# Two-bank PSUM tiles in a fused attention and rational feed-forward kernel on one Trainium2 core

## The chip, the cores and the metric

The kernel runs on one core of one Trainium2 chip. The metric is the device time of one execution in microseconds; lower is better. Three runs of the kernel before gave 1387.79, 1389.79 and 1392.57 us, median 1389.79. The profile is that of one further execution.

The engines are named as the profile names them: PE multiplies matrices (PEld is its load of the stationary operand), DVE is the vector engine, ACT the scalar engine, POOL the general engine that cannot see PSUM, SP issues the DMAs. PSUM is the buffer that PE writes into: eight banks of 512 fp32 a partition.

## The reference

Causal attention by blocks of 64, for 8 batches of 8 heads with 576 positions of 64 elements, then a feed-forward layer over the 4608 tokens of 512 elements (2048 hidden), whose nonlinearity is a quotient of two polynomials:

```python
scores = scale * np.matmul(q, k.transpose(0, 1, 3, 2))
mask = block_i >= block_j                      # blocks of 64 positions
scores = np.where(mask, scores, -1000000000.0)
scores = scores - np.max(scores, axis=-1, keepdims=True)
attn = np.exp(scores)
attn = attn / (np.sum(attn, axis=-1, keepdims=True) + 1e-09)
attn_out = np.matmul(attn, v)

h = x @ w_in
P = a[0] + a[1] * h + a[2] * h2 + a[3] * h3    # h2 = h*h, h3 = h2*h
Q = 1.0 + np.abs(b[0]) * np.abs(h) + np.abs(b[1]) * h2
out = (P / (Q + 1e-6)) @ w_out
```

## The kernel before

**Number format.** All operands of the matmuls are fp32r. Each is split into a high part, rounded by ACT, and a low part, the rest, mostly subtracted by DVE or POOL; a product is three matmuls (low x high, high x high, high x low), for scores two over a contraction of 128 rows in which both parts are stacked.

**Order.** The program is traced in one order, by hand, and the framework's planner then fixes the order of every engine's queue at build time, from a simulated timeline and the buffers that are free in it. On the chip each queue is executed in that fixed order, each instruction waiting for its semaphores. So an instruction that is traced late can run early: the first weight block is traced at step 9 but starts at 14 us in the trace.

**Attention.** The unit is a pair of heads, 32 in all; `load(p)` brings q, k and v. `prep(p, which)` transposes q or k (six transposes of 96 rows, L354, in two groups of three, each in its own bank), copies the high part with ACT (L358) and subtracts the low part with DVE (L359); DMAs then lay `kq` out for each head. `vprep(p)` splits v into `vpad`, where 64-column blocks of the two heads lie with gaps of zeros: four ACT copies and four POOL subtractions (L381, L382), two of them for the first 64 keys and two over 256 columns.

The queries are cut into five tiles `t` of 64, 128, 128, 128 and 128 rows, whose keys are the first 64, 192, 320, 448 and 576. A step of the loop `attn_steps` is one tile of one head, so a pair takes ten steps and all attention 320:

- `scores(p, t, j)`: two matmuls (L420, L421) and, on the last block, a small one that adds the mask (L424), into a bank of `ps_a`. Tile 4 has 576 columns, more than a bank holds, and is done in two halves of 288 in two banks. DVE takes the negated maximum of each bank (L425); for tile 4 L428 joins the two maxima.
- `expo(p, t, j)`, one step later: ACT's exp with the maximum as bias and the row's sum as accumulator (L437, which shows as an ACTIVATE and a reading of the accumulator), twice for tile 4. With the second head POOL joins tile 4's two sums (L443), adds 1e-9 (L444), DVE inverts (L445), and POOL scales: the first 64 keys of both heads into `pk` (L446), the rest in place in `pt` (L450).
- `transp(p, t)`, nine steps after the tile's second score: 1, 3, 5, 7 or 9 transposes (L469) in groups with a bank each, of sizes 1; 1, 2; 1, 4; 4, 3; 3, 3, 3. ACT copies a group's high part (L474), DVE subtracts the low part (L475). Tile 0 has 64 rows, so its transpose works on 64 rows and its tile `pt` serves as `pk` too.
- `pv(p, g)`, a step after tiles 2 and 4 have been transposed: the second product (15 matmuls over tiles 0 to 2, 27 over tiles 3 and 4, L488) into one bank of `ps_a`, evicted by ACT and DVE (L491, L492) and written to `xscr` in DRAM.

**Banks.** `ps_a` has five banks, `ps_h` one for the hidden activations, `ps_o` two (tags `o0` and `o1`) for the FFN's output. Scores and `pv` always take `ps_a`. Transposes ask `bank(p, ...)`, which for the first four pairs goes round `ps_a`, `o0`, `o1` and `ps_h`, since the FFN isn't running yet, and later takes `ps_a`.

**Weights.** `split_weights` splits the weights in 32 blocks of 128 x 512 with exact integer work: ACT's absolute value (L127), a maximum with a tiny constant on POOL (L128), six DVE operations (L130 to L137), an ACT conversion (L139), a POOL product (L143 or L145). Twenty blocks belong to the first part of the hidden units (phase 0), twelve to the second, kept in DRAM till it starts.

**Feed-forward.** Tokens are taken in 18 blocks of 256, hidden units two at a time: phase 0 has 5 such units a block, phase 1 has 3. `first` is 24 matmuls into a two-part bank h (L200) and the start of the polynomials; `recip` makes the quotient (for phase 1 its reciprocal `r0` is a bank of `ps_a`); `split` the two parts of g; `second` 12 matmuls (L249) that accumulate into `self.o`, two tiles of one bank, over the units of a block. At a block's end phase 0 copies the two halves with ACT (L256) to DRAM; phase 1 adds them to that partial result with two DVE operations (L262) and writes the output. In phase 1, h alternates between `ps_h` and `ps_a`. FFN's units are fed in between the steps of attention from step 53 on, when the first batch is there; what is left runs after attention ends.

## Time and profile before

| what | value |
|---|---|
| median of three runs | 1389.79 us |
| the profiled execution, and its span | 1388.67 us, 1386.9 us |
| mean granted clock of PE | 0.971 |
| PE, PEld busy | 1296.0, 1190.8 us |
| DVE, ACT, POOL busy | 1031.0, 909.3, 958.3 us |
| first matmul of the FFN's h | 133.4 us |
| last score matmul of attention begins | at about 961 us |

The profile's page gives each engine's busy time as a union of its instructions' spans. Matmuls are pipelined, so their spans overlap and a busy PE need not be one at its full rate; the count of matmuls in a stretch of time says more. The page cuts the span in 40 slices of 34.7 us; these are its rows for the engines (tenths of the slice that are busy, 9 standing for 90% or more) and for the clock:

```profile
PE   4778799999899989999999999999989999999998
DVE  5898877787678868877767777766756677777665
POOL 4888987687677757777767676766556655556564
PEclk9687999999999999999999999999999999999999
```

The chain of waits, followed back from the last instruction, is 70% PE, 9% DVE, 8% POOL, 5% ACT and 4% DMA. In the groups of instructions, a row has the line, engine, operation, output and inputs, shapes and count, then the busy time in us, the mean of one in ns, and the idle time of the engine ahead of them with what ended it.

### The profile page before, as it was taken

What the parts mean: (1) busy time and instruction counts of PE and PEld (TensorE: products, weight loads), DVE (VectorE), ACT (ScalarE), POOL (GpSimd) and SP (SyncE); (2) the same over time, 40 slices, a digit from 0 to 9 for tenths busy, and PEclk for the clock granted to TensorE, in tenths of its full rate; (3) what the DMA queues carried; (4) which work ended last, traced back from release to release, by engine and by line L of the source; (5) the groups of instructions that cost most, each with busy time, mean ns of one, the idle gap of its engine ahead of it and who ended that gap; (6) DMA issues with size and microseconds to landing.
All of it is one profiled execution on the core that took longest, in us unless ns stands there. A gap on an engine that the chain in (4) does not pass through costs nothing.

```text
span 1386.9 us, 25820 instructions
## 1 busy us (share of the span) xinstructions
PE 1296.0 (93%) x8736; PEld 1190.8 (86%) x8736; DVE 1031.0 (74%) x2048; ACT 909.3 (66%) x2250; POOL 958.3 (69%) x1240
## 2 busy tenths in 40 slices
PE   4778799999899989999999999999989999999998
PEld 3667788999888889888989999999979999999897
DVE  5898877787678868877767777766756677777665
ACT  5766766777577766776777777776545655555553
POOL 4888987687677757777767676766556655556564
PEclk9687999999999999999999999999999999999999
DMA  9778555666556665675654565651711333333332
GB/s 221 191 195 236 147 150 160 168 168 181 147 136 154 163 167 140 156 171 140 168 134 110 153 149 126 150 141 44 263 55 61 107 122 122 122 122 122 122 122 91
DMA packets 225635, 200.93 MB, mean 145 GB/s; under 512 B 132064, under 2 KB 195552, under 8 KB 225504
## 3 DMA queue, kind: packets, MB, share of 16 engines
q1 hardware_dynamic: 225440, 199.28, 53.8%
q8 instruction: 70, 1.15, 0.3%
q14 instruction: 61, 0.50, 0.1%
q0 software_dynamic: 64, 0.00, 0.0%
HBM read 98.57 MB, written 44.04 MB: 103 GB/s over the span
## 4 chain that ended last, share of the span: by engine, by line
PE 70%; DVE 9%; POOL 8%; ACT 5%; DMA 4%; issue 2%; SPq 1%; POOLq 0%; ACTq 0%; DVEq 0%
PE h L200 25%; PE o L249 25%; PE o L488 9%; PE t L469 4%; PE s L420 3%; PE s L421 3%; PE tp L354 2%; ACT p L437 1%; DVE v L224 1%; POOL u L210 1%; DVE nm L425 1%; POOL p L450 1%; DMA x<-xscr 1%; POOL gl L233 1%; DVE u L223 1%
## 5 line engine op out<-in xcount | busy, mean ns | idle before, releaser
L200 PE MATMUL h<-x,wih 128*128 128x256 f32 x2304 | 442.6, 288 | 10.1 <-DMA x<-xscr 5.9
L200 PEld LDWEIGHTS h<-x,wih 128*128 128x128 f32 x2304 | 368.8, 192 | 19.6 <-issue 6.8
L200 PE MATMUL h<-x,wil 128*128 128x256 f32 x1152 | 329.5, 286 | 0.0
L249 PE MATMUL o<-woh,gl 128*128 128x512 f32 x576 | 233.0, 405 | 8.1 <-POOL gl L233 6.8
L209 POOL TENSOR_SCALAR v<-u,bab 128x512 f32<-128x512 f32 x144 | 119.7, 831 | 162.9 <-ACT u L207 160.8
L249 PE MATMUL o<-woh,gh 128*128 128x512 f32 x576 | 228.5, 397 | 0.0
L249 PE MATMUL o<-wol,gh 128*128 128x512 f32 x576 | 227.2, 395 | 0.0
L233 POOL TENSOR_TENSOR gl<-s,gh 128x512 fp32r<-128x512 f32 x144 | 188.4, 1309 | 51.4 <-ACT gh L232 48.3
L425 DVE TENSOR_REDUCE nm<-s 128x1 f32<-128x288 f32 (+4 forms) x384 | 161.7, 427 | 81.2 <-PE s L424 46.1
L200 PEld LDWEIGHTS h<-x,wil 128*128 128x128 f32 x1152 | 221.3, 192 | 0.5
L437 ACT ACTIVATE p<-s,nm 128x288 f32<-128x288 f32 (+4 forms) x384 | 184.6, 485 | 48.4 <-DVE nm L425 34.9
L210 POOL TENSOR_TENSOR u<-v,u 128x512 f32<-128x512 f32 x144 | 189.7, 1318 | 9.8
L450 POOL TENSOR_SCALAR p<-p,rc 128x128 f32<-128x128 f32 (+3 forms) x256 | 166.2, 660 | 30.0 <-DVE rc L445 28.3
L217 ACT ACTIVATE v<-u,qcb 128x512 f32<-128x512 f32 x144 | 104.6, 726 | 95.9 <-POOL u L210 95.1
L207 ACT ACTIVATE u<-h 128x512 f32<-128x512 f32 x144 | 86.0, 597 | 120.8 <-PE h L200 114.4
L420 PE MATMUL s<-kq 128*128 128x256 f32 (+3 forms) x384 | 138.3, 362 | 22.0 <-DMA kq<-hl 9.6
L211 DVE TENSOR_TENSOR s<-s,h 128x512 f32<-128x512 f32 x144 | 98.6, 684 | 68.7 <-ACT s L208 67.9
L249 PEld LDWEIGHTS o<-woh,gl 128*128 128x128 f32 x576 | 109.5, 190 | 28.9 <-POOL gl L233 9.3
L249 PEld LDWEIGHTS o<-wol,gh 128*128 128x128 f32 x576 | 109.1, 189 | 22.8
L249 PEld LDWEIGHTS o<-woh,gh 128*128 128x128 f32 x576 | 109.5, 190 | 16.0
L421 PE MATMUL s<-kq 128*128 128x256 f32 (+3 forms) x384 | 121.0, 317 | 0.0
L469 PE MATMUL t<-ident,p 128*128 128x128 f32 (+1 forms) x672 | 114.0, 280 | 6.2 <-DVE x L492 1.8
(105 smaller groups left out, 3031.9 us busy)
## 6 DMA issues: line engine op xcount, KB each, us to landing
kq<-hl SPq DMA_DIRECT2D x64, 432.0 KB, 4.2
x<-xscr SPq DMA_DIRECT2D x96, 256.0 KB, 3.6
kq<-hl SPq DMA_DIRECT2D x64, 288.0 KB, 5.3
xscr<-x SPq DMA_DIRECT2D x32, 320.0 KB, 4.2
qr<-in_q_dram SPq DMA_DIRECT2D x64, 144.0 KB, 2.8
kr<-in_k_dram SPq DMA_DIRECT2D x64, 144.0 KB, 2.9
kq<-hl SPq DMA_DIRECT2D x64, 144.0 KB, 4.8
pscr<-os SPq DMA_DIRECT2D x18, 512.0 KB, 3.2
```

The costliest lines, as they stand in the source:

```text
L200: nc.tensor.matmul(h[:, j, :], lhsT=w[:, dc, fs], rhs=xs[dc // 2][:, dc % 2, hl, :], start=(dc == 0 and i == 0), stop=(dc == 3 and i == 2))
L209: nc.gpsimd.tensor_scalar(out=vt, in0=ut, scalar1=b1, scalar2=b0, op0=ALU.mult, op1=ALU.add)
L210: nc.gpsimd.tensor_tensor(out=ut, in0=vt, in1=ut, op=ALU.mult)
L233: nc.gpsimd.tensor_tensor(out=gl.rearrange("p j t -> p (j t)"), in0=st, in1=gh.rearrange("p j t -> p (j t)").bitcast(F32), op=ALU.subtract)
L249: nc.tensor.matmul(self.o[m], lhsT=g[:, j, ms], rhs=w[:, f, :], start=(u == 0 and j == 0 and i == 0), stop=(u == nu - 1 and j == 1 and i = ...
L420: nc.tensor.matmul(ps[:, :ww], lhsT=kq[:, 0, qs], rhs=kq[:, 1, c0:c0 + ww], start=True, stop=False)
L421: nc.tensor.matmul(ps[:, :ww], lhsT=kq[:, 0, qs], rhs=kq[:, 2, c0:c0 + ww], start=False, stop=not last)
L425: nc.vector.reduce_max(out=nm[:nq, j, i:i + 1], in_=ps[:nq, :w], axis=AX.X, negate=True)
L437: nc.scalar.activation(out=pt[:nq, j, c0:c0 + w], in_=banks[i][:nq, :w], func=AF.Exp, bias=nm[:nq, j, 0:1], scale=1.0, accum_out=sm[:nq, j ...
L450: nc.gpsimd.tensor_scalar(out=pt[:nq, jj, 64:n], in0=pt[:nq, jj, 64:n], scalar1=rc[:nq, jj:jj + 1], scalar2=1.0, op0=ALU.mult, op1=ALU.mult)
L469: nc.tensor.transpose(ps[:, i, :nq], src, ident[:nq, :nq])
L488: nc.tensor.matmul(o[:, s0:w], lhsT=vblock(vv, x), rhs=pp, start=(x == 0 and i == 0), stop=(x == nb - 1 and i == 2))
```

## The change

The eight banks are dealt out anew: `ps_a` three banks, a new pool `ps_w` one tile of two banks, `ps_h` one, `ps_o` one tile of two banks. `wide(p, ...)` hands out two-bank tiles: for the first four pairs `ps_w` and `ps_o` in turn, later `ps_w` alone. `bank` goes to `ps_a` three times in four and to `ps_h` once for the first four pairs, and to `ps_a` later.

With that,

- prep's six transposes go into one wide tile, with one ACT copy and one DVE subtraction of 576 columns where there were two of 288;
- tile 4's scores go into one wide tile: one maximum over both banks, one exp with one sum; L428 and L443 go;
- `transp` works in groups of 1; 1, 2; 1, 4; 7; 5, 4, where those of 7 and 5 are wide;
- v's blocks of the two heads are split by one ACT copy and one POOL subtraction of 512 columns;
- tile 0's transpose takes 128 rows, of a tile `p0` that lasts, whose lower half is zeroed once;
- FFN's `self.o` is one tile, copied or added in one operation;
- L128 and L444 on POOL get a second operation that changes nothing (a second maximum with the same constant, a product with 1.0).

```diff
-    ps_a = ctx.enter_context(tc.tile_pool(name="ps_a", bufs=5, space=PSUM))
+    ps_a = ctx.enter_context(tc.tile_pool(name="ps_a", bufs=3, space=PSUM))
+    ps_w = ctx.enter_context(tc.tile_pool(name="ps_w", bufs=1, space=PSUM))
...
-            nc.gpsimd.tensor_scalar_max(at, at, WMIN)
+            nc.gpsimd.tensor_scalar(out=at, in0=at, scalar1=WMIN, scalar2=WMIN, op0=ALU.max, op1=ALU.max)
...
-                self.o = [ps_o.tile([128, DM], F32, name=f"o{ph}_{c}_{m}", tag=f"o{m}")
-                          for m in range(2)]
+                self.o = ps_o.tile([128, 2, DM], F32, name=f"o{ph}_{c}", tag="o")
...
-                    for m in range(2):
-                        nc.scalar.copy(out=osb[:, m, :], in_=self.o[m])
+                    nc.scalar.copy(out=osb, in_=self.o)
...
-                    for m in range(2):
-                        nc.vector.tensor_tensor(out=osb[:, m, :], in0=self.o[m], in1=part[:, m, :], op=ALU.add)
+                    nc.vector.tensor_tensor(out=osb, in0=self.o, in1=part, op=ALU.add)
...
+        p0 = apers.tile([128, 2, 64], F32, name="p0")
+        nc.vector.memset(p0[64:128], 0.0)
...
-            for half in range(2):
-                ps = bank(p - 1, f"tp{p}_{which}_{half}")[:, :3 * LP].rearrange("p (c t) -> p c t", c=3)
...
+            ps = wide(p - 1, f"tp{p}_{which}")
+            for c in range(6):
+                nc.tensor.transpose(ps[:, c // 3, LP * (c % 3):LP * (c % 3 + 1)],
+                                    raw[:, c].rearrange("p j d -> p (j d)"), ident[:LP, :LP])
+            pf = ps[:, :, :3 * LP]
+            h2, l2 = (x.rearrange("p (c t) -> p c t", c=2) for x in (h, l))
+            nc.scalar.activation(out=h2, in_=pf, func=AF.Copy, scale=sc)
+            nc.vector.scalar_tensor_tensor(out=l2, in0=pf, scalar=sc, in1=h2.bitcast(F32),
+                                           op0=ALU.mult, op1=ALU.subtract)
...
-                  lambda x: x[:, 128:].rearrange("p (b c) -> p b c", c=192)[:, :, 0:64],
-                  lambda x: x[:, 128:].rearrange("p (b c) -> p b c", c=192)[:, :, 128:192]]
-            of = [vr[0:64, 0:1], vr[64:128, 0:1], vr[:, 1:9:2], vr[:, 2:9:2]]
+                  lambda x: x[:, 128:].rearrange("p (b s d) -> p b s d", s=3, d=D)[:, :, 0:3:2, :]]
+            of = [vr[0:64, 0:1], vr[64:128, 0:1], vr[:, 1:9].rearrange("p (b s) d -> p b s d", s=2)]
...
-                pool, tag = ((ps_a, "a"), (ps_o, "o0"), (ps_o, "o1"), (ps_h, "a"))[nbank[0] % 4]
+                pool, tag = ((ps_a, "a"), (ps_h, "a"))[nbank[0] % 4 == 3]
...
+        def wide(p, name):
+
+            if p < LEND:
+                nbank[1] += 1
+                pool, tag = ((ps_w, "w"), (ps_o, "o"))[nbank[1] % 2]
+            else:
+                pool, tag = ps_w, "w"
+            return pool.tile([128, 2, 512], F32, name=name, tag=tag)
...
+            ps = (wide(p, f"s{p}_{t}_{j}") if t == 4 else
+                  ps_a.tile([128, 512], F32, name=f"s{p}_{t}_{j}", tag="a").unsqueeze(1))
...
-                nc.vector.reduce_max(out=nm[:nq, j, i:i + 1], in_=ps[:nq, :w], axis=AX.X, negate=True)
-                banks.append(ps)
-            if t == 4:
-                nc.vector.tensor_tensor(out=nm[:, j, 0:1], in0=nm[:, j, 0:1], in1=nm[:, j, 1:2], op=ALU.min)
...
+            sc = ps[:nq, :n, :w] if n > 1 else ps[:nq, 0, :w]
+            nc.vector.tensor_reduce(out=nm[:nq, j:j + 1], in_=sc, axis=AX.XY if n > 1 else AX.X, op=ALU.max,
+                                    negate=True)
...
-            for i, (c0, w) in enumerate(pieces(t)):
-                nc.scalar.activation(out=pt[:nq, j, c0:c0 + w], in_=banks[i][:nq, :w], func=AF.Exp,
-                                     bias=nm[:nq, j, 0:1], scale=1.0, accum_out=sm[:nq, j, i:i + 1])
+            px = pt[:nq, j].rearrange("q (i k) -> q i k", i=2) if t == 4 else pt[:nq, j]
+            nc.scalar.activation(out=px, in_=sc, func=AF.Exp, bias=nm[:nq, j:j + 1], scale=1.0,
+                                 accum_out=sm[:nq, j:j + 1])
...
-            if t == 4:
-                nc.gpsimd.tensor_tensor(out=sm[:, :, 0], in0=sm[:, :, 0], in1=sm[:, :, 1], op=ALU.add)
-            nc.gpsimd.tensor_scalar_add(rc[:nq], sm[:nq, :, 0], 1e-9)
+            nc.gpsimd.tensor_scalar(out=rc[:nq], in0=sm[:nq], scalar1=1e-9, scalar2=1.0, op0=ALU.add, op1=ALU.mult)
...
-            groups = {1: [1], 3: [1, 2], 5: [1, 4], 7: [4, 3], 9: [3, 3, 3]}[nb]
+            groups = {0: [1], 1: [1, 2], 2: [1, 4], 3: [7], 4: [5, 4]}[t]
...
+                if gn > 4:
+                    ps = wide(p, f"t{p}_{t}_{gi}").rearrange("p b (c t) -> p (b c) t", c=4)
...
-                    nc.tensor.transpose(ps[:, i, :nq], src, ident[:nq, :nq])
+                    nc.tensor.transpose(ps[:, i, :], src, ident)
```

39 lines of the change are left out of this document (15 added, 24 removed).

## The prediction, before the changed kernel was run

> **What bounds the kernel now.** The page's head gives the span and each engine's busy time:
>
> ```profile
> span 1386.9 us, 25820 instructions
> ...
> PE 1296.0 (93%) x8736; PEld 1190.8 (86%) x8736; DVE 1031.0 (74%) x2048; ACT 909.3 (66%) x2250; POOL 958.3 (69%) x1240
> ```
>
> PE's 93% mixes stages with different limits, so the table of stages comes next. Columns: window in us, its length, then busy us and instruction count of PE, PEld, DVE, ACT, POOL, then granted clock, DMA share, GB/s.
>
> ```profile
> core 0: us, PE busy (x) PEld busy (x) DVE busy (x) ACT busy (x) POOL busy (x), PEclk, DMA share, GB/s
> 25.00:175.00 150.00, 113.33 (x673) 101.62 (x674) 132.53 (x301) 106.52 (x315) 131.29 (x173) 0.82 0.74 194
> 175.00:700.00 525.00, 500.47 (x3536) 464.14 (x3535) 410.10 (x886) 372.39 (x1018) 392.21 (x556) 0.98 0.62 157
> 700.00:1000.00 300.00, 297.59 (x2146) 278.34 (x2145) 218.50 (x467) 215.16 (x560) 200.55 (x298) 1.00 0.53 138
> 1000.00:1100.00 100.00, 94.23 (x578) 84.88 (x577) 62.58 (x84) 53.79 (x88) 62.18 (x51) 0.97 0.24 80
> 1100.00:1300.00 200.00, 200.00 (x1277) 181.95 (x1276) 140.79 (x202) 110.09 (x178) 118.81 (x108) 1.00 0.41 127
> ```
>
> From 25 to 175 us attention runs almost alone, with weight splitting filled in: DVE is busy 132.53 of 150 us (88%), POOL 131.29 (88%), PE 76%. Here the vector engines set the pace. From 175 on, PE is the bound: 95%, then 99%, and 100% in the FFN-only stage. Time taken off DVE, ACT or POOL is therefore worth time before 175 us, and afterwards only as far as it shortens PE's stalls, 24.5 us between 175 and 700. Those stalls, from the view of waits of PE in that window (who waited, for whom, us in total, times, longest):
>
> ```profile
> PE o L488 <- DVE pt0l L475: 6.0, 4, 2.1
> PE h L200 <- DMA x<-xscr: 5.2, 3, 2.6
> PE tp L354 <- ACT p L437: 3.7, 3, 1.6
> PE o L249 <- POOL gl L233: 3.4, 5, 1.1
> PE t L469 <- ACT p L437: 1.7, 3, 1.1
> ```
>
> The third and the fifth are waits of transposes for an exp of other data, that is, for a PSUM bank: 5.4 us, small with the present banks.
>
> How much of the changed work lies in the first stage? L428, the second step of the split maximum, runs twice per pair of heads, L128 once per weight block. The same stage for L428 alone, then for L128 alone:
>
> ```profile
> 25.00:175.00 150.00, 4.31 (x12) 0.82 0.74 194
> ```
> ```profile
> 25.00:175.00 150.00, 29.47 (x19) 0.82 0.74 194
> ```
>
> So six of the 32 pairs and 19 weight blocks lie in the first stage, and 26 pairs after it.
>
> **The change part by part.** Durations by form (groups by line, shapes kept apart; busy us, mean ns of one):
>
> ```profile
> L425 DVE TENSOR_REDUCE nm<-s 128x1 f32<-128x288 f32 x128 | 56.3, 450 | 38.2 <-PE s L421 19.9 <-PE s L424 17.9
> L425 DVE TENSOR_REDUCE nm<-s 128x1 f32<-128x448 f32 x64 | 39.1, 616 | 6.1 <-PE s L424 5.9
> L425 DVE TENSOR_REDUCE nm<-s 128x1 f32<-128x192 f32 x64 | 22.2, 350 | 12.2 <-PE s L424 11.9
> L428 DVE TENSOR_TENSOR nm<-nm 128x1 f32<-128x1 f32 x64 | 22.4, 350 | 0.5
> L359 DVE SCALAR_TENSOR_TENSOR hl<-tp,hl 128x288 fp32r<-128x288 f32 x128 | 55.7, 449 | 13.6 <-ACT hl L358 7.9 <-DMA qr<-in_q_dram 2.9 <-DMA sto<-in_moe_w_out_dram 2.3
> L475 DVE TENSOR_TENSOR pt2l<-t,pt2h 128x384 fp32r<-128x384 f32 x128 | 68.7, 546 | 3.9 <-ACT pt2h L474 3.8
> L475 DVE TENSOR_TENSOR pt2l<-t,pt2h 128x512 fp32r<-128x512 f32 x32 | 21.8, 682 | 2.2 <-ACT pt2h L474 2.1
> L474 ACT CAST pt2h<-t 128x512 fp32r<-128x512 f32 x32 | 18.8, 586 | 5.3 <-PE t L469 5.2
> L437 ACT ACTIVATE p<-s,nm 128x288 f32<-128x288 f32 x128 | 62.9, 498 | 13.1 <-DVE nm L428 12.7
> L437 ACT ACTIVATE p<-s,nm 128x448 f32<-128x448 f32 x64 | 41.1, 644 | 12.4 <-DVE nm L425 12.3
> L437 ACT ACTIVATION_READ_ACCUMULATOR p<-s,nm 128x1 f32 x320 | 65.4, 204 | 0.0
> L128 POOL TENSOR_SCALAR wao<-wao 128x512 f32<-128x512 f32 x16 | 24.7, 1543 | 0.9 <-ACT wao L127 0.5
> L209 POOL TENSOR_SCALAR v<-u,bab 128x512 f32<-128x512 f32 x144 | 119.7, 831 | 162.9 <-ACT u L207 160.8
> L382 POOL TENSOR_TENSOR vpl<-vr,vph 128x256 fp32r<-128x256 f32 x64 | 52.3, 833 | 23.6 <-PE o L488 17.6 <-ACT vph L381 4.0 <-DMA kq<-hl 1.1
> L233 POOL TENSOR_TENSOR gl<-s,gh 128x512 fp32r<-128x512 f32 x144 | 188.4, 1309 | 51.4 <-ACT gh L232 48.3 <-PE s L424 2.4
> L443 POOL TENSOR_TENSOR sm<-sm 128x2 f32<-128x2 f32 x32 | 7.7, 240 | 13.5 <-ACT p L437 13.5
> ```
>
> *Maximum, DVE.* The reduce grows by (616 - 350)/256 = 1.04 ns an element, so one over 576 takes about 616 + 128 x 1.04 = 749 ns. It replaces 450 + 450 + 350 = 1250 ns, twice a pair: 1.00 us (at worst, were its two rows priced apart, only the minimum's 0.35 would go each time).
> *Prep, DVE.* The L475 rows lie on one line with L359: (682 - 546)/128 = 1.06 ns an element, so 576 take 750 instead of 898 ns, twice a pair: 0.30 us.
> *Transposes' subtractions, DVE.* Tile 3: 682 + 546 becomes 896 elements, about 1089; tile 4: 3 x 546 becomes 640 and 512 elements, 818 + 682. Together 0.28 us.
> That is 1.58 us a pair as durations. Neighbours overlap, though (timeline of DVE: start, union of both, count):
>
> ```profile
> 311.08 1.02 DVE L475 TENSOR_TENSOR pt2l<-t,pt2h 128x384 fp32r<-128x384 f32 x2
> 320.11 0.81 DVE L425 TENSOR_REDUCE nm<-s 128x1 f32<-128x288 f32 x2
> ```
>
> Two of 546 ns take 1.02 us, two of 450 take 0.81, so about 0.08 us of each merged operation was already hidden. Six merges a pair (2 reduces, 2 preps, 2 subtractions) cost 0.48 of the saving: 1.10 us is the lower bound. The Trainium skill (Perfetto Trace Analysis, section Optimizing Scalar/DVE Operations) says that a profiled latency holds about twice the engine's own fixed cost and gives some 125 ns for DVE on PSUM; by it six merges would bring an estimated 0.75 us, beside the 0.70 for the two removed minimums.
>
> *Exp, ACT.* An element costs (644 - 498)/160 = 0.91 ns, so (498 + 204) x 2 becomes about 644 + 128 x 0.91 + 204 = 965, saving 0.44 us, twice a pair; the other merged copies save less. ACT is 71% busy in the first stage and bounds nothing.
> *POOL.* L128 gets a second, idle operation. The trace has the one-operation form at 1543 ns and a two-operation form of the same size, L209, at 831. I take L209's price, 0.71 us less, as the nearest row. The other bounds are no change, and 0.71 more if each operation costs a pass of its own. v's pair of 833 becomes one of about 1309 (L233's size): 0.36; L443 goes: 0.24. L444's new form has no 2-element row to compare with; zero. Per pair 0.60 us.
> *Transposes of tile 0* over 128 rows: no more instructions, and
>
> ```profile
> L469 PE MATMUL t<-ident,p 64*128 64x64 f32 x32 | 8.8, 275 | 0.1
> L469 PE MATMUL t<-ident,pk 128*128 128x128 f32 x128 | 37.9, 296 | 4.2 <-POOL pk L446 1.8 <-ACT p L437 1.7 <-DVE x L492 0.5
> ```
>
> 32 x 21 ns = 0.7 us at most; nothing if only the rate of issue counts. The new memset runs once.
> *FFN's output tile.* One eviction replaces two, and cannot start before the second half is summed. In mid-kernel 24 matmuls of the next h (2.87 us) stand between it and the tile's next writer, against an add of two halves that takes 1.38:
>
> ```profile
> 1096.28 2.87 PE h L200 x24
> 1381.68 1.38 DVE L262 TENSOR_TENSOR os<-o,pt 128x512 f32<-128x512 f32 x2 [4.48 <-PE o L249]
> ```
>
> So it is hidden there (uncovered it would be some 0.5 us for each of 36 blocks); at the end of the kernel, where nothing covers it, I count +0.5 us. FFN's h and r0 now share three ps_a banks instead of five.
>
> ```profile
> L223 DVE SCALAR_TENSOR_TENSOR u<-u,r 128x512 f32<-128x512 f32 x54 | 37.2, 688 | 64.5 <-ACT r L222 64.5
> ```
>
> r0 is held for an exp (about 0.7 us for 512 by the rows of L437) and three DVE operations of this row's kind, some 2.8 us and the gaps between them, of a unit's period of 5.6 us (1277 matmuls in 200 us, 36 a unit). I count nothing.
>
> *Sum.* First stage: 6 pairs x 1.10 to 1.58 us = 6.6 to 9.5 us of DVE; at its share of 0.88 that is 7.5 to 10.8 us. POOL loses 19 x 0.71 + 6 x 0.60 = 17.1 us, or 19.5 of time, so it leaves its place as co-bound and DVE decides: 9 us. After 175 us PE's stalls on DVE, ACT and POOL shrink with their load (perhaps 1 to 2 us of 24.5), and waits for banks grow by about as much; I set these against each other. End +0.5. Total -8.5 to -9 on the profiled execution's 1388.67 us (span 1386.9 and 1.8 around it): about 1380. The shown median, 1389.79, is 1.1 higher; against it the forecast is 0.7% down.
>
> **The rivals.**
> *A wait for the wide buffer (slower).* From the fifth pair on there is one two-bank buffer beside ps_a's three, where five single banks served before. Scores of tile 4 for head 1 need it while head 0's are still being reduced and exponentiated (749 + 965 ns), and head 0's need it from the five transposes of the pair before (640 elements: a copy of 586 + 128 x 0.91 = 0.70 us, a subtraction of 0.82). PE's queue is in order: whatever stands behind such a matmul, FFN's included, waits. Against it: between the two scores the program puts 27 matmuls of the second product,
>
> ```profile
> 227.57 3.23 PE o L488 x27
> ```
>
> 3.23 us, and the order of the queues is worked out with the buffers known. The wait decides as soon as less than 1.7 us (some 14 such matmuls) stands between. With 1.7 + 1.5 us in each of 26 pairs the full price is 83 us; a quarter uncovered costs 21, less the 9 gained: about 1401. (A slower two-operation form on POOL, 19 x 0.71 - 3.6 = 10 us of work, 11 of time, would end at 1400 as well.) The Trainium skill speaks for this rival (Perfetto Trace Analysis, sections Matmuls and Optimizing Scalar/DVE Operations): independent groups should rotate through different banks so that one's evacuation overlaps the next's matmuls, and instructions should be broken up where unsaturated engines cause bubbles. The 5.4 us of bank waits above do not yet show it.
> *No gain.* The first stage is not limited by DVE's sum but by latencies between engines and by DMA (74% there), or the two-operation form on POOL is no faster: then POOL, at 88%, saves only 6 x 0.60 = 3.6 us of work, 4 of time, and the end costs 0.5: 1385.2. Together 1385 to 1393, centre 1388.
> *More gain.* DVE and POOL are both relieved, so the stage ends with POOL's saving as well, and half of PE's 24.5 us of stalls goes: -9 - 12 = about 1368.
>
> **How the numbers follow.** Forecast (1374 to 1385.5) 0.42; more gain 0.20; no gain 0.20; wide-buffer wait 0.18 (the POOL loss in it at 0.02). Within 0.3% (4.2 us) is about what a measurement of this kernel cannot tell from no change, so faster is 0.42 + 0.20 = 0.62, same 0.20, slower 0.18. The range of 8 in 10 takes the forecast, no gain, nearly all of more gain and the milder part of the slower case: 1362 to 1398.
>
> **What would show it.** Right: L128 near 0.8 us; one reduce of 576 near 0.75 and one exp near 0.76; the sixth pair done some 9 us earlier; PE's windows after it as dense as now (about 673 matmuls per 100 us to 700, 715 after). Wrong: PE waiting for ACT p or DVE nm ahead of the scores by more than 15 us in all; DVE still at 88% with the first stage no shorter; FFN-only stage below 100%.

## The result, and the profile after

The changed kernel is slower: a median of 1442.99 us in four runs (1440.68 to 1445.07), beside 1391.18 us for the kernel before in the same session. The ratio is **1.037 [1.034, 1.040]**, some 52 us. The forecast was 1380 us with a range to 1398. One execution of a kernel tried below, `pv_in_wide`, took 3051.86 us where its other three took 1608 to 1609, and is left out of the ratio.

The page's head of the profiled execution after (1443.59 us), its span and the busy time of each engine:

```profile
span 1441.8 us, 25123 instructions
...
PE 1303.8 (90%) x8736; PEld 1197.6 (83%) x8736; DVE 1005.1 (70%) x1775; ACT 887.4 (62%) x1944; POOL 947.0 (66%) x1176
```

The work did shrink: DVE is busy 25.9 us less, ACT 21.9, POOL 11.3, with 697 instructions fewer. PE has the same 8736 matmuls and is busy 7.8 us longer, at a granted clock of 0.958 instead of 0.971. The span grew by 54.9 us, so PE is idle 138.0 us where it was 90.9: 47.1 us more. The table of stages after, with the same windows and columns as before, says where:

```profile
25.00:175.00 150.00, 104.25 (x631) 94.79 (x631) 124.10 (x249) 99.48 (x256) 130.63 (x159) 0.80 0.75 195
175.00:700.00 525.00, 478.81 (x3302) 442.62 (x3302) 371.33 (x705) 338.82 (x799) 361.74 (x485) 0.96 0.58 147
700.00:1000.00 300.00, 285.45 (x2042) 265.47 (x2041) 201.77 (x392) 202.19 (x474) 189.86 (x281) 0.99 0.53 129
...
1100.00:1300.00 200.00, 199.89 (x1282) 182.20 (x1281) 145.12 (x192) 113.41 (x183) 122.69 (x108) 1.00 0.35 111
```

Window less PE's busy time gives the idle time: 45.8 us in the first stage (36.7 before), 46.2 from 175 to 700 (24.5), 14.6 from 700 to 1000 (2.4). Of the 47.1 us, 42.9 lie in these three. The last row, FFN alone, is as full as it was. So the loss is spread over all of attention, and in these three stages no engine is busier than before.

What PE waited for ahead of the scores, over the whole span (line waiting, released by: us in total, times, longest), before:

```profile
PE s L420 <- DMA kq<-hl: 9.6, 4, 4.7
PE s L420 <- ACT p L437: 5.3, 9, 1.0
PE s L420 <- DVE pt0l L475: 2.0, 1, 2.0
PE s L420 <- DVE pt2l L475: 1.6, 2, 0.8
```

and after, where L429 is the old L420 and L483 the old L475:

```profile
PE s L429 <- DMA kq<-hl: 25.1, 11, 5.3
PE s L429 <- DVE pt2l L483: 12.8, 10, 3.3
PE s L429 <- DVE pt0l L483: 11.3, 9, 3.4
PE s L429 <- DVE x L500: 6.5, 3, 5.4
PE s L429 <- ACT p L445: 4.5, 6, 1.3
```

A score matmul reads only `kq`. Where it waits for the subtraction `pt2l` or `pt0l` of another tile's transposes, or for the eviction `x`, it waits for the PSUM bank that this operation was the last to read. Those bank waits are 12.8 + 11.3 + 6.5 + 4.5 = 35.1 us, against 5.3 + 2.0 + 1.6 = 8.9 us among the rows shown of before. Which banks they are for is seen when the same matmuls are parted by form:

```profile
L429 PE MATMUL s<-kq 128*128 128x288 f32 x128 | 40.3, 329 | 13.7 <-DVE pt2l L483 12.8 <-DVE rc L451 0.7
L429 PE MATMUL s<-kq 128*128 128x256 f32 x128 | 45.7, 360 | 39.3 <-DMA kq<-hl 25.1 <-DVE pt0l L483 11.1 <-ACT p L445 2.8
L429 PE MATMUL s<-kq 128*128 128x448 f32 x64 | 26.9, 420 | 6.9 <-DVE x L500 6.3 <-ACT p L445 0.6
```

The form with 288 columns is tile 4's, the only scores in a wide tile: 12.8 us of the 35.1 are waits for a wide tile. The other 22.3 us are of scores of tiles 0 to 3, and so waits for the three single banks.

The waits for DMAs grew by more than these. Those for `kq` itself are up by 15.5 us; the other rows of PE with a DMA, three before and three after:

```profile
PE h L200 <- DMA x<-xscr: 5.9, 4, 2.6
PE tp L354 <- DMA kr<-in_k_dram: 4.5, 4, 1.7
PE tp L354 <- DMA qr<-in_q_dram: 3.8, 1, 3.8
...
PE h L201 <- DMA x<-xscr: 14.7, 5, 4.0
PE tp L354 <- DMA kr<-in_k_dram: 9.2, 5, 3.4
PE tp L354 <- DMA qr<-in_q_dram: 5.4, 2, 4.3
```

All DMA waits of PE together rose from 23.8 to 54.4 us, by 30.6, while other rows fell (the second product's waits for `pt0l` and `pt1l` from 9.7 to 2.9). Prep, whose output is copied to `kq`, itself uses the wide tile, so these waits too may come from the banks; how a transfer comes late was not traced.

The timeline after shows the wait for the wide tile twice (start, union of the rows joined, engine, operation, count, and in brackets the idle time before it):

```profile
330.48 0.27 PE L477 MATMUL t<-ident,pk 128*128 128x128 f32 x1
...
330.59 0.60 PE L477 MATMUL t<-ident,p 128*128 128x128 f32 x4
...
331.34 0.68 ACT L482 CAST pt2h<-t 128x640 fp32r<-128x640 f32 x1
332.06 0.82 DVE L483 TENSOR_TENSOR pt2l<-t,pt2h 128x640 fp32r<-128x640 f32 x1 [0.76 <-ACT pt2h L482]
332.94 0.40 PE L429 MATMUL s<-kq 128*128 128x288 f32 x1 [1.75 <-DVE pt2l L483]
...
498.65 1.18 ACT L482 CAST pt2h<-t 128x640 fp32r<-128x640 f32 x2 [1.38 <-PE t L477]
...
499.82 0.60 DVE L435 TENSOR_REDUCE nm<-s 128x1 f32<-128x448 f32 x1
...
500.35 0.68 DVE L225 SCALAR_TENSOR_TENSOR v<-u,v 128x512 f32<-128x512 f32 x1
...
500.94 0.68 DVE L138 SCALAR_TENSOR_TENSOR wpo<-sto,wpo 128x512 int32<-128x512 int32 x1
...
501.55 1.42 DVE L483 TENSOR_TENSOR pt2l<-t,pt2h 128x640 fp32r<-128x640 f32 x2
...
502.42 0.40 PE L429 MATMUL s<-kq 128*128 128x288 f32 x1 [0.62 <-DVE pt2l L483]
```

At 330 us the five transposes of tile 4 are followed on PE by nothing but the next pair's scores of tile 4, which need the same wide tile: PE stands for 1.75 us while ACT copies and DVE subtracts. At 498 us other matmuls lie between, but the subtraction itself is late: the copies are done at 499.83 at the latest, but DVE works in order, first does a reduce, an FFN operation and one on a weight block, and begins the subtraction at 501.55. Counted in the trace over the 26 pairs from the seventh on, the five-transpose tile is held 3.19 us on average, of which 0.71 are the transposes, 0.40 a wait for ACT, 0.69 the copy, 0.56 a wait for DVE and 0.82 the subtraction.

The start of each pair's first scores, in us (pairs are numbered from 0); the last two columns belong to experiments below:

| pair | before | after | narrow_tile4 | pool_ops_alone |
|---|---|---|---|---|
| 4 | 109.9 | 109.1 | 110.1 | 104.9 |
| 10 | 287.8 | 304.8 | 292.0 | 284.2 |
| 18 | 543.4 | 577.7 | 552.0 | 527.4 |
| 30 | 904.8 | 964.5 | 929.6 | 884.2 |

Up to pair 4, while two wide tiles are in use (`ps_w` and `ps_o`), nothing is lost and nothing gained. From there to pair 30, with one wide tile, a pair takes (964.5 - 109.1)/26 = 32.9 us instead of 30.6.

### The profile page after: what moved, and what is told of

It is laid out like the page before. It is cut to its first block, busy times and chain, and to the rows that moved or that the text cites. A ratio compares the mean times of both kernels' runs of the same rounds, so it can differ in the third digit from the quotient of the medians.

```text
span 1441.8 us, 25123 instructions
## 1 busy us (share of the span) xinstructions
PE 1303.8 (90%) x8736; PEld 1197.6 (83%) x8736; DVE 1005.1 (70%) x1775; ACT 887.4 (62%) x1944; POOL 947.0 (66%) x1176
## 4 chain that ended last, share of the span: by engine, by line
PE 69%; DVE 8%; DMA 8%; POOL 6%; ACT 4%; issue 2%; SPq 2%; ACTq 0%; DVEq 0%; POOLq 0%
PE o L249 25%; PE h L201 25%; PE o L496 8%; DMA kq<-hl 4%; PE t L477 4%; PE s L429 3%; PE s L430 3%; PE tp L354 1%; DMA xscr<-x 1%; DVE pt2l L483 1%; DMA x<-xscr 1%; POOL p L456 1%; DMA sto<-in_moe_w_out_dram 1%; DVE nm L435 1%; POOL u L211 1%
## 5 line engine op out<-in xcount | busy, mean ns | idle before, releaser
L201 PE MATMUL h<-x,wih 128*128 128x256 f32 x2304 | 442.0, 289 | 23.4 <-DMA x<-xscr 14.7
L234 POOL TENSOR_TENSOR gl<-s,gh 128x512 fp32r<-128x512 f32 x144 | 191.8, 1333 | 77.4 <-ACT gh L233 76.0
L435 DVE TENSOR_REDUCE nm<-s 128x1 f32<-128x576 f32 (+4 forms) x320 | 153.4, 484 | 126.5 <-PE s L433 79.1
L445 ACT ACTIVATE p<-s,nm 128x576 f32<-128x576 f32 (+4 forms) x320 | 169.0, 529 | 49.9 <-DVE nm L435 48.5
L429 PE MATMUL s<-kq 128*128 128x288 f32 (+3 forms) x384 | 136.2, 362 | 61.5 <-DMA kq<-hl 25.1
L456 POOL TENSOR_SCALAR p<-p,rc 128x128 f32<-128x128 f32 (+3 forms) x256 | 162.5, 646 | 30.7 <-DVE rc L451 29.3
L429 PEld LDWEIGHTS s<-kq 128*128 128x128 f32 x384 | 77.4, 202 | 74.2 <-issue 24.2
L430 PE MATMUL s<-kq 128*128 128x288 f32 (+3 forms) x384 | 120.2, 319 | 0.0
```

The source lines that it names most:

```text
L201: nc.tensor.matmul(h[:, j, :], lhsT=w[:, dc, fs], rhs=xs[dc // 2][:, dc % 2, hl, :], start=(dc == 0 and i == 0), stop=(dc == 3 and i == 2))
L234: nc.gpsimd.tensor_tensor(out=gl.rearrange("p j t -> p (j t)"), in0=st, in1=gh.rearrange("p j t -> p (j t)").bitcast(F32), op=ALU.subtract)
L429: nc.tensor.matmul(ps[:, i, :ww], lhsT=kq[:, 0, qs], rhs=kq[:, 1, c0:c0 + ww], start=True, stop=False)
L430: nc.tensor.matmul(ps[:, i, :ww], lhsT=kq[:, 0, qs], rhs=kq[:, 2, c0:c0 + ww], start=False, stop=not last)
L435: nc.vector.tensor_reduce(out=nm[:nq, j:j + 1], in_=sc, axis=AX.XY if n > 1 else AX.X, op=ALU.max, negate=True)
L445: nc.scalar.activation(out=px, in_=sc, func=AF.Exp, bias=nm[:nq, j:j + 1], scale=1.0, accum_out=sm[:nq, j:j + 1])
```

## The experiments

The theory after the result was that the new deal of PSUM banks costs everything, and within it the single wide tile; the rivals were that three single banks are too few, that one of the parts that need no bank is to blame (POOL's second operation, v's merge, tile 0), or that any edit redraws the planner's queues by this much. Each ratio is against the kernel before, run beside it on the same chip.

### Which part: banks, or the rest

`banks_alone` is the changed kernel with the three bank-free parts undone:

```diff
-            nc.gpsimd.tensor_scalar(out=at, in0=at, scalar1=WMIN, scalar2=WMIN, op0=ALU.max, op1=ALU.max)
+            nc.gpsimd.tensor_scalar_max(at, at, WMIN)
...
-            nc.gpsimd.tensor_scalar(out=rc[:nq], in0=sm[:nq], scalar1=1e-9, scalar2=1.0, op0=ALU.add, op1=ALU.mult)
+            nc.gpsimd.tensor_scalar_add(rc[:nq], sm[:nq], 1e-9)
...
-                  lambda x: x[:, 128:].rearrange("p (b s d) -> p b s d", s=3, d=D)[:, :, 0:3:2, :]]
+                  lambda x: x[:, 128:].rearrange("p (b c) -> p b c", c=192)[:, :, 0:64],
+                  lambda x: x[:, 128:].rearrange("p (b c) -> p b c", c=192)[:, :, 128:192]]
...
-                    nc.tensor.transpose(ps[:, i, :], src, ident)
+                    nc.tensor.transpose(ps[:, i, :nq], src, ident[:nq, :nq])
```

> The changed kernel with the three bank-free parts taken back (POOL's second operations, v's blocks in one operation, tile 0's 128 rows): what is left is the new deal of the banks and the merged operations. If banks are the main cause, 30 us or more above before, and the rest of the 52 us is what the bank-free parts cost (up to 16). If the bank-free parts are the main cause, within 15 us of before.

1445.64 us, 1.039 [1.036, 1.042]: the whole loss is there with the new deal of the banks and the merged operations that it serves. These two were not parted.

`old_pool_ops` undoes only the first two lines of that diff in the changed kernel.

> The changed kernel with POOL's two operations (the maximum of the weight blocks, the 1e-9 on the sums) in their old one-operation forms. The maximum took 1.96 to 2.04 us in the changed kernel against 1.54 before, 32 times: 16 us of POOL, 9 of them in the first stage. Theory 3 expects 10 to 16 us less than the changed kernel, theories 1 and 2 less than 5 us.

1439.86 us, 1.035 [1.032, 1.038], which overlaps the changed kernel's 1.037. Next, the other way round, the bank-free parts on the kernel before. `pool_ops_alone` adds the second operations there, `vblocks_alone` v's merge, `tile0_alone` the 128 rows with `p0`, and `no_psum_parts` all of these, with the product by 1.0 as L128's second operation:

```diff
-            nc.gpsimd.tensor_scalar_max(at, at, WMIN)
+            nc.gpsimd.tensor_scalar(out=at, in0=at, scalar1=WMIN, scalar2=1.0, op0=ALU.max, op1=ALU.mult)
```

> The kernel before with the second operation on POOL's maximum and on the 1e-9, as in the change, and nothing else. The bank-free parts together cost 16 us over before (run no_psum_parts). If POOL's longer maximum is what costs (32 x 0.46 us = 15 us of POOL, some 19 of the blocks in the first stage, where POOL is as busy as DVE), this run is 8 to 16 us above before. If the price is that any edit draws another order of the queues from the planner, whatever its own cost (theory 4), this run and the next two scatter within 10 us on either side without regard to their work.

> The kernel before with v's blocks of both heads split in one operation. Work taken off: 0.19 us of ACT and 0.3 us of POOL a pair. By work alone: 0 to 3 us faster than before. If merging is bad because the later, longer operation releases v's tile late and holds up the loads behind it in SP's queue, 5 us or more slower. Theory 4: anything within 10 us on either side.

> The kernel before with tile 0's transposes over 128 rows of a lasting tile. Work added: 32 x 0.02 us of PE at most. By work alone: the same within 1 us. Theory 4 (the planner's order changes and with it the waits): 3 to 10 us to either side, which is then the size of the noise that any edit carries here.

> The kernel before with those parts of the change that need no bank: v's blocks in one operation, tile 0's transposes over 128 rows, the second operation on the 1e-9; and on the weight blocks' maximum a second operation of another kind, a product with 1.0 in place of a second maximum. All theories expect it within 5 us of before or up to 5 us faster. The duration of the maximum tells what its price hangs on: about 0.8 us if two operations have a fast path whatever they are, about 1.5 if a maximum alone costs that, 2.0 if each added operation costs half a microsecond.

| kernel | median us | ratio to before |
|---|---|---|
| pool_ops_alone | 1387.33 | 0.999 [0.997, 1.001] |
| tile0_alone | 1386.60 | 0.998 [0.996, 1.000] |
| vblocks_alone | 1400.03 | 1.007 [1.005, 1.010] |
| no_psum_parts | 1407.41 | 1.012 [1.009, 1.015] |

POOL's second operations cost nothing and tile 0 nothing that can be told apart from that. v's merge, which takes work away from ACT and POOL, costs 0.7% on the kernel before. Why stays open: PE's waits for `kq` ahead of the scores are 19.3 us there against 9.6, but `pool_ops_alone` has 19.7 and loses nothing. The three together are no sum of the single ones either (1.2%); none of the theories had expected the 16 us of `no_psum_parts`. Edits of little work thus move this kernel by up to about 1%. The planner's order is the likely reason, which is not shown, and smaller differences between two of these variants are read as nothing. In L128 the groups of `no_psum_parts` show a second operation by another function at the same price:

```profile
L128 POOL TENSOR_SCALAR wai<-wai 128x512 f32<-128x512 f32 x16 | 32.2, 2014 | 5.5 <-ACT wai L127 5.1
```

2014 ns, against 1.54 us with one operation and about 2000 with two maxima.

### What a bank is worth

`four_banks` and `three_banks` are the kernel before with one or two banks left unused:

```diff
-    ps_a = ctx.enter_context(tc.tile_pool(name="ps_a", bufs=5, space=PSUM))
+    ps_a = ctx.enter_context(tc.tile_pool(name="ps_a", bufs=3, space=PSUM))
```

> The kernel before with ps_a cut from five banks to four, one bank left unused. Three banks cost 212 us. If the price of a bank grows steeply as they run out (theory 1, a queue for few servers), the first one taken costs far less than the second: 20 to 70 us of the 212. If it is a step at three, below 10 us; if it is linear, about 105 us.

> The kernel before with ps_a cut from five banks to three and two banks left unused; every operation is as before. If the loss comes from having too few independent banks (theory 1), this alone loses most of it: 30 us or more over the kernel before. If it comes from the one two-bank tile that prep, tile 4's scores and the large groups of transposes share (theory 2), three banks do without harm: within 10 us of before. If it is POOL's slower operation L128 (theory 3): within 5 us of before.

1459.59 us, 1.051 [1.049, 1.054], with four; 1602.51 us, 1.153 [1.150, 1.155], with three. The fifth bank is worth 5.1%, the fourth a further 10. PE's waits in `three_banks`:

```profile
PE s L420 <- ACT p L437: 20.7, 31, 1.9
PE t L469 <- ACT p L437: 17.1, 30, 1.6
```

Scores and transposes wait for an exp of other data, the kind of bank wait that the prediction had seen as 5.4 us (of prep and the transposes, 175 to 700 us) and put down as small. So the change gives away two single banks, worth 15% as long as every user needs them, and gets most of it back by the users that move to the wide tile, to end at 3.7%. How full the banks are, counted from each one's first matmul to its last reader between 250 and 900 us: before, all five singles are held at once for 12.5% of the time; in `three_banks` all three for 37%; in the changed kernel all three for 18%, and the wide tile for 58%.

`pooled_banks` and `pooled_after` give the bank of `ps_h` to `ps_a`, so that FFN's h and attention share six banks, or four (part of `pooled_after`'s edit):

```diff
-    ps_a = ctx.enter_context(tc.tile_pool(name="ps_a", bufs=3, space=PSUM))
+    ps_a = ctx.enter_context(tc.tile_pool(name="ps_a", bufs=4, space=PSUM))
...
-    ps_h = ctx.enter_context(tc.tile_pool(name="ps_h", bufs=1, space=PSUM))
...
-        self.pools, self.hpools = [ffn], [ps_h]
+        self.pools, self.hpools = [ffn], [ps_a]
```

> The kernel before with the hidden activations' own bank ps_h given to ps_a: six banks that scores, transposes, second products and h all share, and no other edit. If single banks are what PE runs short of, sharing them helps: 3 to 15 us faster than before. If h loses its bank to attention while the FFN needs it, or the waits of before for banks (5.4 us of PE) are all there is to gain, within 5 us of before or slower.

> The changed kernel with ps_h given to ps_a in the same way: four single banks that h shares, the wide tile as it is. Theory 1 (too few single banks) expects a gain of 15 us or more over the changed kernel, since the bank of h stands free for part of each unit; theory 2 (the wide tile is what is waited for) expects within 8 us of the changed kernel.

1424.46 us, 1.025 [1.023, 1.028], and 1438.14 us, 1.036 [1.034, 1.038]. Sharing the bank makes the kernel before worse and the changed one no better. Why is not shown: h may lose its bank to attention while the FFN needs it, as the first expectation says, and what attention gains and what h loses were not parted. So these runs don't show that the changed kernel has single banks enough.

### Which user of the wide tile

`pv_in_wide` loads the wide tile further, with the second product's accumulator:

```diff
-            o = ps_a.tile([128, 512], F32, name=f"o{p}_{g}", tag="a")
+            o = wide(p, f"o{p}_{g}")[:, 0, :]
```

> The changed kernel with the second product's accumulator taken from the wide tile in place of ps_a: two of the 16 single banks per pair that are asked for, and those held longest, move over to the wide tile, which then has eight users per pair in place of six. Theory 1 expects it to be faster than the changed kernel (5 to 20 us); theory 2 expects it to be 20 us or more slower.

1608.97 us, 1.159 [1.156, 1.162]: two more uses a pair, and the kernel is another 12 points slower, though two of a pair's uses of single banks are gone. The wide tile can't take them. The next kernels take a user away. `narrow_transposes` returns the transposes of tiles 3 and 4 to single banks (groups of 4, 3 and 3, 3, 3), `narrow_scores` returns tile 4's scores, with two maxima and two exps as before, and `narrow_tile4` returns tile 4's transposes alone:

```diff
-            groups = {0: [1], 1: [1, 2], 2: [1, 4], 3: [7], 4: [5, 4]}[t]
+            groups = {0: [1], 1: [1, 2], 2: [1, 4], 3: [7], 4: [3, 3, 3]}[t]
```

> The changed kernel with the groups of transposes as they were (4, 3 and 3, 3, 3 in single banks); prep and tile 4's scores stay wide. Theory 2 (the wide tile is contended) expects 20 us or more less than the changed kernel, because two of its six users per pair go and the waits of scores for pt2l with them (29 us in the changed kernel). Theory 1 (too few single banks) expects it to be slower still by 5 to 20 us, because three more tiles per pair now ask for ps_a's three banks.

> The changed kernel with tile 4's scores as before: two single banks of ps_a, two maxima, two exps. The wide tile keeps prep and the two large groups of transposes. If the handing over of the wide tile from the pair before's transposes to the next pair's scores is the loss, this removes it, and the kernel gains 15 us or more. If the three single banks are the scarcer resource, four more claims per pair on them cost more than that frees: 10 us or more slower than the changed kernel.

> The changed kernel with only tile 4's transposes back in three single banks (3, 3, 3); tile 3's seven stay wide. In the trace of the changed kernel 11 of 20 pairs between 250 and 900 us have scores of tile 4 start within 0.3 us of the release of the wide tile by these transposes. If that handover is the main loss: 10 us or more faster than the changed kernel. If single banks are scarcer: 5 to 15 us slower, like the run with all large groups narrow.

| kernel | out of the wide tile | median us | ratio to before |
|---|---|---|---|
| narrow_transposes | transposes of tiles 3 and 4 | 1458.17 | 1.049 [1.047, 1.051] |
| narrow_scores | scores of tile 4 | 1471.56 | 1.060 [1.057, 1.063] |
| narrow_tile4 | transposes of tile 4 | 1408.35 | 1.016 [1.013, 1.019] |

Two of the three are worse than the change, since what leaves the wide tile falls on three scarce single banks: PE's waits ahead of the transposes, 16.7 us after the change, are 43.7 and 38.8 there. The third gives back 2.2 of the 3.7%, about 30 us. It is the user whose release the next pair's scores of tile 4 await, as at 330 us above. PE's waits in `narrow_tile4` ahead of the scores:

```profile
PE s L429 <- DMA kq<-hl: 16.6, 5, 7.3
PE s L429 <- ACT p L445: 14.7, 13, 3.6
...
PE s L429 <- DVE x L500: 4.6, 5, 1.2
...
PE s L429 <- DVE pt2l L483: 1.2, 1, 1.2
PE s L429 <- DVE pt0l L483: 0.8, 1, 0.8
```

The waits for the wide tile (`pt2l`) fell from 12.8 us after the change to 1.2. Those for single banks hardly changed in sum, 20.1 us against 22.3: `pt0l` fell from 11.3 to 0.8, the exp rose from 4.5 to 14.7. PE's waits for DMAs fell from 54.4 to 35.6 us. (The 29 us in the first of these expectations add waits of PE and of PEld for `pt2l`, 12.8 and 16.3, which overlap.) Of the successions on the wide tile between 250 and 900 us, 15 of 118 follow within 0.3 us in the changed kernel, 11 of them from tile 4's transposes to the next pair's tile-4 scores, at 11 of the 20 pairs in that stretch; in `narrow_tile4` that kind is gone, and 8 of some 100 are left. The stage from 175 to 700 us fills up again, though not to before's 500.47 us:

```profile
175.00:700.00 525.00, 488.32 (x3448) 451.94 (x3447) 383.73 (x751) 352.74 (x851) 384.96 (x509) 0.98 0.60 152
```

Two more from there. `tile4_old_v` also takes back v's merge and L128's second operation; `tile4_prep_narrow` also takes prep out of the wide tile, two halves in two single banks as before:

```diff
-            ps = wide(p - 1, f"tp{p}_{which}")
...
+            for half in range(2):
+                ps = bank(p - 1, f"tp{p}_{which}_{half}")[:, :3 * LP].rearrange("p (c t) -> p c t", c=3)
```

> The changed kernel with tile 4's transposes in three single banks (which took 35 us off it), and with v's blocks in two operations and the weight blocks' maximum in its one-operation form, as before. v's blocks alone cost 10 us in the kernel before. If the costs add, this comes to 1396 to 1401 us, 8 to 12 above before. If v's cost there was a matter of that order of the queues alone, it stays near 1408.

> The changed kernel with tile 4's transposes and prep in single banks; the wide tile is left to tile 3's transposes and tile 4's scores, three users a pair in place of six. If the wide tile is still the scarcer resource after tile 4's transposes have left it, this is 5 to 15 us faster than that step alone (1408). If now the three single banks are, it is 15 us or more slower, as when tile 4's scores or all large groups moved to them.

1410.45 us, 1.014 [1.012, 1.017], the same as `narrow_tile4`; so v's 0.7% isn't to be had here. And 1478.37 us, 1.064 [1.061, 1.066]: prep is worth having in the wide tile, by nearly 5%. The 1.4 to 1.6% that `narrow_tile4` still lacks were not traced to one user. Its 20.1 us of waits for single banks, against 8.9 before, point to the three single banks; the wide tile's other handovers and the order of the queues are candidates too. So both halves of the new deal are short: the wide tile, where one user's leaving gives back over half of the loss, and the single banks, which take back that one user and none of the others tried.

### Moving the handover in the program

If the handover is bad because tile 4's transposes and the next pair's scores are traced side by side, then tracing the transposes two steps earlier, seven steps after a tile's scores in place of nine, should part them. `lag7_after` does that, and `lag7_before` is its control on the kernel before:

```diff
-ALAG3 = 10
+ALAG3 = 7
...
-        LAST = ALAG3 + 3
+        LAST = 13
```

> The changed kernel with the transposes seven steps after a tile's scores in place of nine: in program order the wide tile is then asked for at steps 3, 4, 5, 6, 8 and 9 of a pair's ten, where it was 3, 5, 6, 8, 8 and 9. No operation and no bank is added or taken. If the collisions on the wide tile are the loss: 10 us or more faster than the changed kernel. If it is the number of banks as such: within 8 us.

> The control of the run above: the kernel before with the same seven steps. It has no wide tile, so the theory of collisions expects no gain: within 8 us of before. If it gains as much as the changed kernel does, the shorter lag helps for another reason.

1499.01 us, 1.080 [1.077, 1.083], and 1406.82 us, 1.013 [1.011, 1.016]. The edit costs the kernel before 1.3% and the changed one 4.3 points. The handover from tile 4's transposes to the next pair's scores no longer follows within 0.3 us, but others do (in `lag7_after` the scores of the two heads, and prep with the transposes of tile 4). So this expectation failed. The edit moves every tile's transposes and the second products, not one step alone, so it doesn't show what that one handover is worth; it shows that with one wide tile for four kinds of user, six uses a pair, a move can bring others together.

## Why the prediction was wrong, point by point

**Which case came.** The slower rival, the wait for the wide buffer, with its chance of 0.18. Its place was named rightly: head 0's scores of tile 4 against the five transposes of the pair before. The loss is 2.3 us a pair from pair 4 on, 32.9 - 30.6, times 26 about 60 us of attention and 52 of the whole. That lies between the quarter that was counted, 21 us, and the full price of 83, but by luck and not by the price's own terms: scores of tile 4 wait 12.8 us for the wide tile, all of it on the pair before's transposes; the handover between the two heads, 1.7 of the 3.2 us, shows no wait at all; and waits for single banks and for DMAs were not in the price. What made it a rival and not the forecast were two steps that failed.

**The step that failed: "waits for banks grow by about as much", 1 to 2 us.** It priced the bank waits of the kernel before (5.4 us) instead of the banks. `four_banks` and `three_banks` show that this small number says nothing of the price of a bank: one bank fewer costs 70 us and two cost 212 us in the same kernel. Where the sum counted 1 to 2 us, the bank waits of the score rows rose from 8.9 to 35.1 us, PE's waits for DMAs, which the sum did not hold at all, by 30.6, and its idle time in all by 47.1. The reading that would have helped is a count: five interchangeable buffers for scores, transposes, prep and product, against three and one, and one long hold where there were shorter ones in separate banks.

**The cover: "the order of the queues is worked out with the buffers known".** The planner does know the buffers, and still placed the handover with nothing between at 330 us, and at 11 of 20 pairs within 0.3 us. The 27 matmuls of cover stand between the two heads' scores; between the transposes and the next scores there is no such thing. The price of 1.5 us for that handover, a copy of 0.70 and a subtraction of 0.82, was right for the two operations (0.69 and 0.82) and left out that ACT and DVE come to them late, by 0.40 and 0.56 us on average, and by over 1 us for DVE in 6 of 26 pairs.

**"Here the vector engines set the pace".** The -9 us of the first stage did not come. DVE's 132.53 us in it became 124.10, but the stage also got less far (631 matmuls instead of 673). Up to the start of pair 4, where both kernels have done the same pairs, DVE is busy 79.5 us instead of 84.9, some 1.4 us a pair less, as sized; yet pair 4 starts at 109.1 instead of 109.9 us, with the two wide tiles still in use. POOL makes the opposite test: some 0.46 us more (2.00 less 1.54) for each of 32 weight blocks, 19 of them in the stage where POOL is 88% busy, cost nothing (`pool_ops_alone`, 0.999). So POOL's 88% was no bound. For DVE this is argued only, since the banks changed at the same time and no run takes work off DVE alone. Beyond this, `pool_ops_alone` reaches pair 30 some 20 us earlier than before and ends within 0.3% of it. What attention gains there is given back later: when its last scores begin, 2496 of the FFN's 5184 matmuls have started, 2625 before, and PE works through the rest.

**L128's second operation.** Predicted as 0.83 us with 0.71 more as the far bound; measured:

```profile
L129 POOL TENSOR_SCALAR wai<-wai 128x512 f32<-128x512 f32 x16 | 32.7, 2044 | 10.1 <-ACT wai L128 10.0
L129 POOL TENSOR_SCALAR wao<-wao 128x512 f32<-128x512 f32 x16 | 31.4, 1961 | 2.5 <-ACT wao L128 2.2
```

About 2.0 us against 1.54, inside the bounds and on the other side of "no change". L209's 0.83 us is not the price of having two operations. Its scalars are columns of a tile and not constants, and it multiplies and adds where L128 takes a maximum; L450, a product with a column and then with a constant, takes 0.79 us for the same size. Whether the column or the function decides, no run tried. As the step bought nothing on either side, the error cost nothing.

**The sizes of the merged operations** were right. Groups after, by form:

```profile
L435 DVE TENSOR_REDUCE nm<-s 128x1 f32<-128x576 f32 x64 | 48.1, 753 | 40.2 <-PE s L433 40.0
L359 DVE SCALAR_TENSOR_TENSOR hl<-tp,hl 128x576 fp32r<-128x576 f32 x64 | 48.1, 751 | 9.7 <-ACT hl L358 9.1
L445 ACT ACTIVATE p<-s,nm 128x576 f32<-128x576 f32 x64 | 47.6, 743 | 17.1 <-DVE nm L435 16.4
L483 DVE TENSOR_TENSOR pt2l<-t,pt2h 128x896 fp32r<-128x896 f32 x32 | 34.7, 1084 | 3.7 <-ACT pt2h L482 3.5
L483 DVE TENSOR_TENSOR pt2l<-t,pt2h 128x640 fp32r<-128x640 f32 x32 | 26.2, 818 | 5.1 <-ACT pt2h L482 5.1
L381 POOL TENSOR_TENSOR vpl<-vr,vph 128x512 fp32r<-128x512 f32 x32 | 44.1, 1379 | 25.4 <-ACT vph L380 25.1
```

The reduce was forecast at 749 ns (753), prep at 750 (751), the subtractions at 1089 and 818 (1084, 818), exp at 761 (743), v at 1309 (1379). The savings were real, and the kernel did not get shorter by them.

**FFN's output tile and its banks** went as said: 1282 matmuls in the FFN-only 200 us, 1277 before, so three `ps_a` banks are enough for h and r0. The eviction is hidden until the end, but for three waits of PE for phase 0's copy, 2.4 us in all. From the last matmul's end to the kernel's it takes 5.1 us, 4.6 before: the +0.5 us came. The last rows of DVE's timeline after:

```profile
1426.94 1.23 DVE L260 TENSOR_TENSOR os<-o,pt 128x1024 f32<-128x1024 f32 x1
...
1436.75 1.22 DVE L260 TENSOR_TENSOR os<-o,pt 128x1024 f32<-128x1024 f32 x1 [6.01 <-PE o L249]
```

Tile 0's 128 rows were free as said.

**The marks.** Of the signs named beforehand, "DVE still at 88% with the first stage no shorter" came only by half (83%, and no shorter). The sign of being right, "the sixth pair done some 9 us earlier", failed: the first scores after six pairs (pair 6) start at 173.6 us instead of 168.1. "PE waiting for ACT p or DVE nm ahead of the scores by more than 15 us in all" did not come as named (4.5 us for `p`); PE waited there for `pt2l`, `pt0l` and `x` instead, on the wide tile at the handover between pairs, and longer on the single banks. The Trainium skill's rules cited in the prediction (Perfetto Trace Analysis, sections Matmuls and Optimizing Scalar/DVE Operations) held for one user: breaking up one merged group, tile 4's transposes, gave back some 30 us. Breaking up others, for which the single banks were short, cost time (`narrow_scores`, `narrow_transposes`, `tile4_prep_narrow`). The Trainium skill (Perfetto Trace Analysis, section Matmul Optimizations) asks for all eight PSUM banks to be in use; `four_banks`, which leaves one idle, agrees at 5.1%.

No kernel tried here beats the one before by a margin that counts; the nearest is `tile0_alone`, 0.2% faster with an interval that ends at 1.000.

## What to carry to other kernels

Before buffers are merged into wider ones, count who uses them, how many of them are interchangeable and how long each user holds one, the wait for the busy engines that release it included; small waits now say nothing about the price of the next buffer, but a run with one buffer fewer does. Time taken off an engine is worth something only if that engine ends the waits, and a share of 88% of a stage isn't proof of that. Where a planner orders the queues, test a part together with an edit of no weight, to know how far the order alone moves the time.

## What the runs showed of the hardware

Two things were not expected. POOL's maximum with one constant took 1.54 us for 128x512 before (up to 1.65 in other runs), with a second constant 1.96 to 2.04 whether the second function was a maximum or a product, while L209's two operations with columns as scalars took 0.83 in the same kernel. And PE's mean granted clock was lower in slower kernels: 0.971 before, 0.958 after, and lower still in the two slowest. Their span and clock, `three_banks` first:

```profile
core 0: 1597.3 us, clock 0.925
```

and `pv_in_wide`:

```profile
core 0: 1606.9 us, clock 0.918
```

In those two PE is busy 1401.3 and 1372.7 us for the same 8736 matmuls that took 1296.0 before. So the loss shows partly as idle time and partly as matmuls that take longer. How much of the second is the clock is not shown: in `four_banks` PE is busy 27.2 us longer than before at a clock of 0.968. The Trainium skill (Perfetto Trace Analysis, section Matmul Optimizations) says that the matmul engine scales its power with its use and should work in unbroken batches; these four clocks agree in direction, but the clock doesn't follow PE's busy share alone (0.967 at 89% in `tile4_prep_narrow`, 0.958 at 90% after).
